# Four reorderings in a long-convolution and token-mixing kernel: weight prefetch, theta products, the pass change and the last stages

## The chip, the cores and the metric

The kernel runs on one core of one Trainium2 chip. Its time is the device time of one execution in microseconds; the median of three runs is given. The profile is one further execution recorded by the hardware profiler, whose span is a few microseconds shorter than the device time. Times inside the profile are counted from the start of that span.

Short names: PE is the matrix engine and PEld its weight loads, DVE the vector engine, ACT the scalar engine, POOL the general engine, SP the engine that here only issues transfers. A bank is one eighth of PSUM, the memory into which matmuls accumulate.

## The reference

A long convolution over the sequence (by FFT), then a token-mixing layer:

```python
# B, S, D = 8, 5696, 128
y = irfft(rfft(x, 2*S) * rfft(h, 2*S))[:, :S, :]        # convolution, per channel
theta = y @ w_theta                                     # [D, D]
zr, zi = y * cos(theta), y * sin(theta)
mix = einsum('ts,bsd->btd', w_tok_r, zr) + einsum('ts,bsd->btd', w_tok_i, zi)   # w_tok: [S, S]
u = y + mix
out = u + max(u @ w_ch, 0)                              # w_ch: [D, D]
```

Nearly all arithmetic is in the two products with the S x S weights, which are stored in float32 and read once each.

## The kernel before

**Convolution and phases.** Stages A to D are an FFT, a product and an inverse FFT in eight groups. In and after the last group, 44 *phase steps* (22 row tiles of 128, two halves of the batch) turn y into z: four transposes bring a tile of y into PSUM, DVE copies it to SBUF (`y_ap`), PE multiplies it by w_theta, ACT takes cosine and sine, DVE multiplies, and SP writes y and z to HBM. The transposes and the theta product use two halves of one PSUM tile `ps`. The first half of the batch reads its y from `ya0`. The second half reads `ya1`, whose last quarter is copied from the SBUF tile `yt` after the last inverse FFT.

```python
def stage_d(st, bp, dh):
    ...
            nc.scalar.activation(y_out, y_in, AF.Copy)
            if n0 + cn == N2:
                for e in range(2):
                    nc.sync.dma_start(yt_hbm[...], yt[64 * e:64 * e + 64]...)
...
def phase_step(ti, hh):
    ps = psum()
    tpz = ps[:, 1, :]...
    for b in range(4):
        nc.tensor.transpose(tpz[:, b, :], yT[:, b, :], ident_bf)
    y_ap = st["sby"].tile([P, 4, D], BF16, tag="y", name="y_ap")
    nc.vector.tensor_copy(y_ap, tpz)                        # DVE reads ps
    nc.sync.dma_start(y2_hbm[ti]..., y_ap...)
    phases_b(ti, y_ap, ..., theta_ps=ps[:, 0, :], tags=None)   # PE writes ps, then ACT, DVE, SP
...
load_ya1(st["yt"])          # after the last group: ya1 <- yt
...
for n, ti in enumerate(tile_order):
    phase_step(ti, 1)
    if n % 4 == 3:
        while len(bts_of[0]) < min(n // 2, NE):
            load_b(0, len(bts_of[0]), bpe)                  # operand blocks of pass 0
```

**Token mixing.** The columns of the weights are split into two passes of 2816, and 64 left over. In each pass the operand is held in SBUF as 11 blocks `b0` to `b10`, each two transfers of 512 KB; the two passes use the same SBUF space. A block holds four original parts (named by the products M2, M6, M7, M5) and three sums (M3, M4, M1). For 22 pairs of row tiles the product is made with seven matmul products in place of eight, so that the operand needs sums; two of the four parts are overwritten by sums as well. Pair 0 of each pass, the "classic" one, uses eight plain products on the original parts, and the sums are formed beside it. A last strip of 64 rows is the pair `None`. It has 88 matmuls for each pass and uses the sums in pass 0, the originals in pass 1.

```python
def sum_b(bt):
    b11, b12, b21, b22 = (bt[q] for q in (M2, M6, M7, M5))
    nc.vector.tensor_sub(bt[M3], b12, b22)
    nc.vector.tensor_sub(bt[M4], b21, b11)
    nc.vector.tensor_add(bt[M1], b11, b22)
    nc.vector.tensor_add(b12, b11, b12)      # in place
    nc.vector.tensor_add(b21, b21, b22)      # in place
...
pairs = (list(range(22)) + [None], [None] + list(range(22)))   # order in pass 0, in pass 1
```

Weights come in six buffers `wb`, each filled by four transfers that POOL issues and that turn float32 into bfloat16. A pair needs four buffers for its first 6 blocks and four for the other 5; a `None` pair needs two and two. DVE transposes them (`wt`) and forms sums of them. The work on a pair is cut into four *stretches* of 3, 3, 3 and 2 blocks.

```python
def load_w(a, row0, p, j0, nj, ng=4):
    wb = wp.tile([P, 4, CJ * 64], BF16, tag="wb")       # 6 buffers
    for i in range(4):
        nc.gpsimd.dma_start(wb[32 * i:32 * i + 32, ...], <weights, float32>)
    return wb
...
ORDER = (M3, M4, M5, M2, M1, M7, M6)                    # products of a pair, in PE's order
if tt is None:
    if first_of_pair:
        ps = [mps.tile(..., tag=f"m{q}") for q in (M3, M4)]         # banks
    ...  # 8 matmuls a block, into ps[0] and ps[1]
    if end_of_pair:
        for h in range(2):
            nc.vector.tensor_add(c[:64], c0[:64], ps[h][:64])       # frees the bank
...
if classic:
    ms = [... tag=f"m{q}" ... for q in range(4)]                    # banks m0 to m3
```

**Background and end.** While PE multiplies in pass 0, the phases of the other half of the rows run beside it. In pass 1 each finished tile gets a *u-stage*: ACT casts (`ub`), PE transposes (`utp`), ACT copies (`uts`), PE multiplies by w_ch (`v`), DVE adds (`c`), SP writes the output. `utp` and `v` share the one bank "misc". The stages still waiting at the end run after the last product:

```python
for _, first, second in spread:
    first()
    second()
```

The order of instructions on each engine is made by a scheduler from this program. It may move an instruction ahead of others on its engine where data allows it.

Of the kernel before, what the change touches and what calls it, by code (L numbers as in the profile page):

```python
# [10 lines left out]
F32 = mybir.dt.float32  # L11
# [11 lines left out]
def kernel(  # L23
# [13 lines left out]
    P = 128  # L37
# [293 lines left out]
    def stage_d(st, bp, dh):  # L331
        def chunk(n0, cn):
            if n0 == 0:
                st["yt"] = fg.tile([P, NB, N2], BF16, tag="yt", name="yt")
            g_, yt = st["g"], st["yt"]
            ps = psum()
            nq = 5 if cn == CN else cn
            for j in range(cn):
                n = n0 + j
                o = ps[:, j // nq, (j % nq) * NB:(j % nq + 1) * NB]  # L340
                for ri in range(2):
                    e_ = e_t[:K1, n, ri, :] if n < EN else e_t[:K1, N2 - n, ri, ::-1]
                    nc.tensor.matmul(o, g_[:K1, ri * N2 + n, :], e_, start=(ri == 0), stop=(ri == 1))  # L343
            y_out = yt[:, :, n0:n0 + cn].rearrange("p m (a q) -> p m a q", q=nq)
            y_in = ps[:, :cn // nq, :nq * NB].rearrange("p a (q m) -> p m a q", q=nq)
            nc.scalar.activation(y_out, y_in, AF.Copy)
            if n0 + cn == N2:
                for e in range(2):
                    nc.sync.dma_start(yt_hbm[dh * HD:(dh + 1) * HD, 2 * bp + e, :],
                                      yt[64 * e:64 * e + 64].rearrange("p m n -> p (m n)"))  # L350
        return [lambda n0=n0, cn=cn: chunk(n0, cn) for n0, cn in CHN]
# [17 lines left out]
    def phases_b(ti, y_ap, b0, nb, yT, sb, th_pool, th_tag, zi_eng, turns=None, tags=("red", "mag"), m=P,  # L369
                 theta_ps=None):  # L370
# [16 lines left out]
        else:  # L387
# [11 lines left out]
            r = theta_ps  # L399
        nc.scalar.activation(mag, r, AF.Abs)  # L400
# [70 lines left out]
    def phase_step(ti, hh):  # L471

        st = sides["phases"]
        yT = st[hh][:, :, ti * P:(ti + 1) * P]
        ps = psum()
        tpz = ps[:, 1, :].bitcast(BF16)[:, :512].rearrange("p (b t) -> p b t", b=4)
        for b in range(4):
            nc.tensor.transpose(tpz[:, b, :], yT[:, b, :], ident_bf)
        y_ap = st["sby"].tile([P, 4, D], BF16, tag="y", name="y_ap")
        nc.vector.tensor_copy(y_ap, tpz)  # L480
        nc.sync.dma_start(y2_hbm[ti].rearrange("p b d -> p (b d)")[:, 512 * hh:512 * hh + 512],
                          y_ap.rearrange("p b d -> p (b d)"))
        phases_b(ti, y_ap, 4 * hh, 4, yT, st["sb1"], None, None, nc.vector, st["turns"], theta_ps=ps[:, 0, :],
                 tags=None)
# [6 lines left out]
    for g, (bp, dh) in enumerate(groups):  # L491
# [15 lines left out]
        woven(b_, (stage_d(st, bp, dh), 0.0, 1.1 if b_ else 1.0), now)  # L507
        if g + 2 == len(groups):
            load_ya1()
    load_ya1(st["yt"])  # L510
# [24 lines left out]
    def sum_b(bt):  # L535
        b11, b12, b21, b22 = (bt[q] for q in (M2, M6, M7, M5))
        nc.vector.tensor_sub(bt[M3], b12, b22)
        nc.vector.tensor_sub(bt[M4], b21, b11)
        nc.vector.tensor_add(bt[M1], b11, b22)
        nc.vector.tensor_add(b12, b11, b12)  # L540
        nc.vector.tensor_add(b21, b21, b22)
# [15 lines left out]
    with tc.tile_pool(name="bpool", bufs=1, reuse_waits="tile") as bp, \  # L557
# [9 lines left out]
        def load_w(a, row0, p, j0, nj, ng=4):  # L567

            wb = wp.tile([P, 4, CJ * 64], BF16, tag="wb")
            for i in range(4):  # L570
                nc.gpsimd.dma_start(  # L571
                    wb[32 * i:32 * i + 32, :ng, :nj * 64],
                    bass.AP(tensor=a.tensor,
                            offset=a.offset + row0 * S + p * H + i * QR + j0 * 64,
                            ap=[[S, 32], [32 * S, ng], [1, nj * 64]]))
            return wb
# [76 lines left out]
        def u_stage(ti, h, c, m):  # L653
            st = {}

            def first():
                ub = ybp.tile([P, 4, D], BF16, tag="yb", name="ub")
                nc.scalar.activation(ub[:m].rearrange("p b d -> p (b d)"), c[:m], AF.Copy)  # L658
                utp = mps.tile([P, 4, P], BF16, tag="misc", name="utp")
                for b in range(4):  # L660
                    nc.tensor.transpose(utp[:, b, :m], ub[:m, b, :], ident_bf[:m, :m])  # L661
                st["uts"] = uts = cp.tile([P, 4, P], BF16, tag="yT", name="uts")
                nc.scalar.activation(uts[:, :, :m], utp[:, :, :m], AF.Copy)  # L663

            def second():
                v = mps.tile([P, 512], F32, tag="misc", name="v")
# [47 lines left out]
        pairs = (list(range(22)) + [None], [None] + list(range(22)))  # L714
# [8 lines left out]
        def loads(k):  # L723
# [6 lines left out]
            else:  # L730
                top, bot = tt * P, H + tt * P
                loaded[k] = [load_w(a, r, p, j0, nj) for a, r in
                             ((moe_w_tok_r, top), (moe_w_tok_i, bot),
                              (moe_w_tok_i, top), (moe_w_tok_r, bot))]

        def prepare(i, at_once=True):
# [8 lines left out]
            w11, w22, w12, w21 = loaded[k]  # L745
# [30 lines left out]
        loads(0)  # L776
        for i, (k, p, tt, j0, s0, nj) in enumerate(stretches):
            first_of_pair = j0 + s0 == 0
# [17 lines left out]
            if tt is None:  # L796


                if first_of_pair:
                    ps = [mps.tile([P, 512], F32, tag=f"m{q}", name=f"m{q}") for q in (M3, M4)]  # L800
# [4 lines left out]
                for j in range(nj):  # L805
                    jj = j0 + s0 + j
                    for r in range(2):
# [3 lines left out]
                        for h, (x0, q0, x1, q1) in enumerate(terms):  # L811
# [3 lines left out]
                                             start=False, stop=sp_)  # L815
                if end_of_pair:
# [11 lines left out]
            if first_of_pair:  # L828
                ms = [mps.tile([P, 512], F32, tag=f"m{q}", name=f"m{q}") for q in range(4 if classic else 7)]
# [20 lines left out]
            if classic:  # L850
# [10 lines left out]
                for j in range(nj):  # L861
                    sum_b(bts[j0 + s0 + j])
# [44 lines left out]
        for _, first, second in spread:  # L907
            first()
            second()
# [30 lines left out]
```

## Time and profile before

| | us |
|---|---|
| device time, median of 3 (2193.06 to 2198.13) | 2196.33 |
| span of the profile | 2192.6 |
| first matmul of pass 0 (line 856) | 555.6 |
| `None` of pass 0 begins | 1323.9 |
| first matmul of pair 0 of pass 1 (line 856) | 1383.7 |
| last vector operation begins | 2188.6 |

The engine rows of the profile give busy time, its share of the span, and the number of instructions. The window rows give, for a stretch of the span, the busy time of each engine (with the number of instructions), the granted share of PE's clock, the mean busy share of the 16 transfer engines (it can exceed 1 where packets of several queues overlap), and GB/s. In the timeline a row has start, length, engine, line, operation and tile; the brackets at its end give how long the engine had been idle before it and what ended this.

The transfer queues, from the page; the last column is the time that the packets of this queue took, as a share of 16 engines over the span:

| queue | what it carries | MB | share |
|---|---|---|---|
| q0 (issued by POOL) | weights, x | 143.00 | 48.6% |
| q1 (issued by SP) | y, z, operand blocks, results | 179.93 | 28.5% |

### The profile page before, as it was taken

The page shows a single profiled execution, that of the slowest core. Times are in us where ns is not written, and L with a number is a line of the kernel's source. Part 1 is how long each engine was busy: PE and PEld are TensorE (multiplying, and loading weights), DVE is VectorE, ACT ScalarE, POOL GpSimd, SP SyncE. Part 2 cuts the span into 40 slices and gives each one's busy share as a digit, 9 for nine tenths or more (in the row PEclk, how much of TensorE's full clock was granted, in tenths as well). Part 3 has the DMA queues.
Part 4 walks back from the last instruction along what each step waited for, and adds up shares of the span by engine and source line. Part 5 has one row for each costly group of instructions (what it writes and reads, how often), then busy time and mean ns, then how long its engine had stood idle before and what let it go on. Part 6 is the DMA issues. An engine that isn't in the chain of part 4 may idle for free.

```text
span 2192.6 us, 41307 instructions
## 1 busy us (share of the span) xinstructions
PE 2018.6 (92%) x15723; PEld 1132.8 (52%) x15723; DVE 1619.2 (74%) x2920; ACT 669.1 (31%) x984; POOL 859.3 (39%) x1568
## 2 busy tenths in 40 slices
PE   4788898756899999999999998899999999999998
PEld 3787888644344444444444443344444444444443
DVE  7766666747878888888877765677777768686866
ACT  5877777656232323323210000011111111111111
POOL 5301010020354544546466462344545353545450
PEclk8698889967999999999999999999999999999998
DMA  6356464588998989999999879677878797979793
GB/s 142 93 132 163 132 143 141 156 183 261 230 171 173 180 166 171 172 176 179 168 171 160 140 113 281 101 128 136 150 133 151 130 154 127 158 127 161 125 155 75
DMA packets 409382, 340.38 MB, mean 155 GB/s; under 512 B 83303, under 2 KB 363751, under 8 KB 408071
## 3 DMA queue, kind: packets, MB, share of 16 engines
q0 software_dynamic: 221312, 143.00, 48.6%
q1 hardware_dynamic: 183552, 179.93, 28.5%
q10 hardware_dynamic: 4320, 14.81, 1.8%
q8 instruction: 123, 2.02, 0.4%
q14 instruction: 75, 0.61, 0.1%
HBM read 381.83 MB, written 97.93 MB: 219 GB/s over the span
## 4 chain that ended last, share of the span: by engine, by line
PE 78%; DMA 7%; DVE 6%; ACT 4%; issue 2%; POOL 1%; SPq 1%; DVEq 0%; ACTq 0%; POOLq 0%
PE m L886 60%; PE m L856 4%; PE ps L320 3%; PE ps L321 3%; PE ps L190 2%; DMA hs<-hf_hbm 2%; DMA wb<-in_moe_w_tok_r_dram 2%; DVE c L893 1%; ACT xs L302 1%; PE ps L343 1%; PE ps L208 1%; DMA y_hbm<-y_ap 1%; PE utp L661 1%; PE v L668 1%; DVE u_t L304 1%
## 5 line engine op out<-in xcount | busy, mean ns | idle before, releaser
L571 POOL DMA_DIRECT2D wb<-in_moe_w_tok_i_dram x720 | 388.7, 547 | 738.7 <-DVE wt L580 660.8
L571 POOL DMA_DIRECT2D wb<-in_moe_w_tok_r_dram x720 | 387.8, 548 | 313.3 <-ACT red L401 165.3
L580 DVE STREAM_TRANSPOSE wt<-wb 128x384 f32<-128x384 f32 (+2 forms) x720 | 360.2, 523 | 125.0 <-PE m L886 67.7
L886 PE MATMUL m<-b,wt 128*128 128x512 bf16 x1848 | 426.8, 379 | 2.4 <-DVE wt L580 2.4
L886 PEld LDWEIGHTS <-wt 128*128 128x128 bf16 x1848 | 180.8, 98 | 220.8 <-DVE wt L580 3.3
L893 DVE TENSOR_TENSOR c<-c,m 128x512 f32<-128x512 f32 x420 | 270.2, 668 | 0.4 <-PE m L886 0.4
L663 ACT ACTIVATE uts<-utp 128x512 bf16<-128x512 bf16 (+1 forms) x90 | 53.3, 592 | 609.7 <-PE utp L661 609.6
L320 PE MATMUL ps<-r_u,u_t 128*128 128x128 f16 x1024 | 136.9, 231 | 16.2 <-DVE u_t L304 10.9
L321 PE MATMUL ps<-r_v,v_t 128*128 128x128 f16 x1024 | 135.6, 230 | 0.0
L658 ACT ACTIVATE ub<-c 128x512 bf16<-128x512 f32 (+1 forms) x90 | 56.3, 628 | 236.7 <-DVE c L824 151.5
L320 PEld LDWEIGHTS <-u_t 128*128 128x128 f16 x1024 | 107.8, 105 | 13.8 <-DVE u_t L304 13.8
L127 POOL DMA_DIRECT2D x<-in_x_dram x64 | 34.2, 540 | 199.2 <-PE ps L190 187.3
L321 PEld LDWEIGHTS <-v_t 128*128 128x128 f16 x1024 | 106.7, 104 | 6.7 <-issue 5.2
L302 ACT ACTIVATE xs<-ps 128x1024 f16<-128x1024 f32 x96 | 94.9, 1015 | 17.7 <-DVE v_t L304 10.3
L304 DVE TENSOR_TENSOR u_t<-xs,hs 128x1024 f16<-128x1024 f16 x96 | 68.4, 712 | 40.0 <-ACT xs L302 26.1
L190 PE MATMUL ps<-f_t,x 89*128 89x180 f16 x512 | 85.1, 312 | 8.3 <-ACT xs L302 6.2
L208 PEld LDWEIGHTS <-w_t 64*128 64x128 f16 x3240 | 64.8, 105 | 37.8 <-issue 24.7
L856 PE MATMUL m<-b,wt 128*128 128x512 bf16 x352 | 79.5, 385 | 0.7 <-ACT mag L400 0.7
L190 PEld LDWEIGHTS <-x 89*128 89x128 f16 x512 | 73.8, 237 | 10.2 <-issue 9.7
L612 ACT ACTIVATE yb<-tpz 128x512 bf16<-128x512 bf16 (+1 forms) x46 | 27.5, 597 | 153.0 <-PE tpz L610 136.1
L382 ACT ACTIVATE red<-theta_ps,magic 128x512 f32<-128x512 f32 (+1 forms) x46 | 31.6, 687 | 137.0 <-PE theta_ps L380 107.9
L304 DVE TENSOR_TENSOR v_t<-xs,hs 128x1024 f16<-128x1024 f16 x96 | 68.4, 713 | 0.0
(2712 smaller groups left out, 3791.5 us busy)
## 6 DMA issues: line engine op xcount, KB each, us to landing
wb<-in_moe_w_tok_r_dram POOLq DMA_DIRECT2D x352, 96.0 KB, 4.5
wb<-in_moe_w_tok_i_dram POOLq DMA_DIRECT2D x352, 96.0 KB, 4.8
wb<-in_moe_w_tok_r_dram POOLq DMA_DIRECT2D x352, 80.0 KB, 4.4
wb<-in_moe_w_tok_i_dram POOLq DMA_DIRECT2D x352, 80.0 KB, 3.8
hs<-hf_hbm SPq DMA_DIRECT2D x192, 128.0 KB, 3.2
cp_hbm<-c SPq DMA_DIRECT2D x88, 256.0 KB, 2.3
c<-cp_hbm SPq DMA_DIRECT2D x88, 256.0 KB, 4.5
out_dram<-c SPq DMA_DIRECT2D x88, 256.0 KB, 4.4
```

Of the source, the lines that this page charges most:

```text
L190: nc.tensor.matmul(ps[:, i // 2, (i % 2) * 2 * K1:(i % 2 + 1) * 2 * K1], lhs(q + i), f1_t[:NB], start=True, stop=True)
L208: nc.tensor.matmul(ps[:, e, j * HD:(j + 1) * HD], w_t2[rows, c0 + j, N2 * (1 - ri):N2 * (3 - ri)], a_st["a"][rows, ri * K1 + c0 + j, :], s ...
L302: nc.scalar.activation(xs[:, :, :, :ck], ps, AF.Copy)
L304: nc.vector.tensor_tensor(uv[r][:, :, :, c0:c0 + ck], xs[:, :, :, :ck], hv[:, r:r + 1, :, :ck].to_broadcast([P, 2, HD, ck]), op=mult)
L320: nc.tensor.matmul(o, u_t[:, at:at + P], r_u, start=True, stop=False)
L321: nc.tensor.matmul(o, v_t[:, at:at + P], r_v, start=False, stop=True)
L571: nc.gpsimd.dma_start(wb[32 * i:32 * i + 32, :ng, :nj * 64], bass.AP(tensor=a.tensor, offset=a.offset + row0 * S + p * H + i * QR + j0 * 6 ...
L580: nc.vector.transpose(wt.rearrange("p j t r -> p (j t r)").bitcast(F32).rearrange("p (j g t) -> p g j t", j=TJ, g=4)[:, :ng, :nj], wb[:, : ...
L658: nc.scalar.activation(ub[:m].rearrange("p b d -> p (b d)"), c[:m], AF.Copy)
L856: nc.tensor.matmul(ms[n // 2 * 2 + h], a[n][:, j, :, r], bts[jj][n % 2 * 2 + h][:, r, :], start=(n % 2 == 0 and jj == 0 and r == 0), stop= ...
L886: nc.tensor.matmul(ms[q], a[q][:, j, :, r], bts[jj][q][:, r, :], start=(jj == 0 and r == 0), stop=(jj == NJ - 1 and r == 1 and q not in left))
L893: nc.vector.tensor_tensor(c, z, ms[q], op=op)
```

## The change

It has four parts. First, the weights of the first pair are not fetched until block `b2` has landed: POOL copies two elements of it into each of these buffers before the load. Pair 0 also fetches its four weights in the order in which it uses them. Second, in a phase step the theta products come before the y copy, and `ya1` is read from `yt` before `yt` itself is written out. Third, at the pass change, `None` of pass 0 goes before pair 21, so that it no longer stands beside `None` of pass 1; the latter has banks m0 and m1 (M2, M6), pair 0 has the banks of M7, M5, M1 and M3; in pass 1 the three sums that overwrite nothing are made during `None`; and in `None` and pair 0 of pass 1 DVE keeps the order of the program. Fourth, the last four u-stages have their own banks and buffers, and all first halves come before all second halves. The aim of all four is that PE waits less between the stages.

```diff
@@ stage_d, phase_step
+                if then is not None:
+                    then(yt)                       # ya1 <- yt, ahead of yt_hbm <- yt
@@ phases_b, after the theta products
+        if copy is not None:
+            copy()
         nc.scalar.activation(mag, r, AF.Abs)
@@ phase_step
-        nc.vector.tensor_copy(y_ap, tpz)
-        nc.sync.dma_start(y2_hbm[ti]...)
+        def copy():
+            nc.vector.tensor_copy(y_ap, tpz)
+            nc.sync.dma_start(y2_hbm[ti]...)
@@ groups
-        woven(b_, (stage_d(st, bp, dh), 0.0, 1.1 if b_ else 1.0), now)
+        woven(b_, (stage_d(st, bp, dh, load_ya1 if last else None), 0.0, 1.1 if b_ else 1.0), now)
-    load_ya1(st["yt"])
@@ load_w
+            if after is not None:
+                nc.gpsimd.tensor_copy(wb[:, 0, :2], after)
@@ loads
-                             ((moe_w_tok_r, top), (moe_w_tok_i, bot),
-                              (moe_w_tok_i, top), (moe_w_tok_r, bot))]
+                after = bts_of[0][2][M2][:, 0, :2] if k == 0 else None
+                ... for n in ((0, 1, 2, 3) if tt == 0 else (0, 3, 1, 2))
@@ sums
-    def sum_b(bt):          # all five sums
+    def sums_apart(bt):     # M3, M4, M1
+    def sums_in_place(bt):  # the two in place
@@ the order of pairs
-        pairs = (list(range(22)) + [None], [None] + list(range(22)))
+        pairs = (list(range(21)) + [None, 21], [None] + list(range(22)))
@@ main loop
+            if (p, tt, j0 + s0) in ((1, None, 0), (1, 1, 0)):
+                if tt is None:
+                    ordered.enter_context(tc.manual_schedule(engines={mybir.EngineType.DVE}))
+                else:
+                    ordered.close()
-                    ps = [... for q in (M3, M4)]
+                    ps = [... for q in ((M2, M6) if p else (M3, M4))]
+                if p == 1:
+                    for j in range(nj):
+                        sums_apart(bts[j0 + s0 + j])          # in None of pass 1
-                ms = [... for q in range(4 if classic else 7)]
+                ms = [... for q in ((M7, M5, M1, M3) if classic else range(7))]
-                    sum_b(bts[j0 + s0 + j])
+                    if p == 0:
+                        sums_apart(bts[j0 + s0 + j])
+                    sums_in_place(bts[j0 + s0 + j])           # in pair 0
@@ the end
-        for _, first, second in spread:
-            first()
+        last = [(f"m{(M3, M5, M4, M2)[n % 4]}", f"m{(M5, M3, M2, M4)[n % 4]}", f"yy{n % 4}") ...]
+        for (_, first, _), tags_ in zip(spread, last):
+            first(tags_)                                     # banks of utp and v, buffer of uts
+        for _, _, second in spread:
             second()
```

## The prediction

> **What bounds the kernel now.** I read the page's engine rows first, then the chain that ended last, then windows of each stage, and last the timeline at the places where PE stood still.
>
> ```profile
> span 2192.6 us, 41307 instructions
> PE 2018.6 (92%) x15723; PEld 1132.8 (52%) x15723; DVE 1619.2 (74%) x2920; ACT 669.1 (31%) x984; POOL 859.3 (39%) x1568
> PEclk8698889967999999999999999999999999999998
> PE 78%; DMA 7%; DVE 6%; ACT 4%; issue 2%; POOL 1%; SPq 1%; DVEq 0%; ACTq 0%; POOLq 0%
> ```
>
> PE is busy for 92% and makes 78% of the chain. In the pairs, from 600 to 1320 us and from 1430 to 2170 us, PE is nearly without a gap, and no part of the change takes work from it there. So the gain must come from three seams: the phases before the first pair, the pass change, and the end. The clock row, in tenths, dips in the first quarter and nearly nowhere after.
>
> The phases, in windows (busy us with counts, then clock, share of the transfer engines, GB/s):
>
> ```profile
> 460.00:470.00 10.00, 4.20 (x46) 2.84 (x44) 5.49 (x11) 6.57 (x12) 7.44 (x14) 0.86 1.11 228
> 470.00:480.00 10.00, 2.10 (x16) 1.39 (x13) 1.88 (x3) 1.78 (x3) 3.81 (x7) 0.50 1.15 259
> 480.00:490.00 10.00, 5.18 (x28) 3.13 (x29) 1.72 (x4) 1.66 (x3) 1.63 (x3) 0.50 0.86 191
> 490.00:500.00 10.00, 8.11 (x73) 5.65 (x71) 7.44 (x15) 7.34 (x14) 0.00 (x0) 0.78 0.58 131
> 530.00:540.00 10.00, 5.07 (x47) 3.43 (x46) 8.21 (x14) 6.84 (x12) 0.00 (x0) 0.84 0.97 324
> ```
>
> From 470 to 490 us every engine rests while transfers are saturated; POOL's instructions there are the weight loads (24 of them start between 459.8 and 483.7 us). After 500 us it is transfers again: y, z and the blocks. The waits of 400 to 600 us say who stood still:
>
> ```profile
> ACT mag L400 <- PE ps L397: 57.1, 15, 15.2
> PE ps L391 <- DVE y_ap L480: 26.5, 14, 6.1
> PEld L478 <- DMA ya<-yt: 9.7, 2, 7.8
> ```
>
> The second row is the theta product that waits for the y copy, the third the second half's wait for `ya1`.
>
> The pass change:
>
> ```profile
> 1330.00:1340.00 10.00, 10.00 (x48) 5.13 (x47) 4.44 (x9) 0.00 (x0) 4.87 (x9) 1.00 1.09 368
> 1340.00:1350.00 10.00, 3.08 (x15) 1.43 (x14) 5.62 (x11) 0.00 (x0) 2.85 (x6) 0.89 1.11 341
> 1370.00:1380.00 10.00, 2.04 (x5) 0.90 (x6) 6.06 (x12) 0.00 (x0) 4.26 (x8) 0.58 0.77 161
> ...
> 1350.05 0.58 PE L812 MATMUL m<-b,wt 128*64 128x512 bf16 x1 [6.97 <-DVE c L824]
> 1373.94 1.50 DVE L580 STREAM_TRANSPOSE wt<-wb 128x384 f32<-128x384 f32 x3 [8.78 <-DMA wb<-in_moe_w_tok_r_dram]
> 1377.95 0.64 PE L814 MATMUL m<-b,wt 128*64 128x512 bf16 x1 [8.67 <-DVE wt L580]
> ```
>
> PE loses 6.97 us because `None` of pass 1 wants the banks of `None` of pass 0, whose addition (L824) stands on DVE behind sums of blocks that are still in flight. It loses 8.67 us because the transposes that it needs stand behind transposes of pair 0, whose weights had not come. At the end, DVE's rows:
>
> ```profile
> 2183.00 0.69 DVE L670 SCALAR_TENSOR_TENSOR c<-v,c 128x512 f32<-128x512 f32 x1 [2.10 <-PE v L668]
> 2185.80 0.69 DVE L670 SCALAR_TENSOR_TENSOR c<-v,c 128x512 f32<-128x512 f32 x1 [2.10 <-PE v L668]
> 2188.59 0.69 DVE L670 SCALAR_TENSOR_TENSOR c<-v,c 128x512 f32<-128x512 f32 x1 [2.10 <-PE v L668]
> ```
>
> One stage each 2.79 us: utp, uts, v and c strictly in turn through the one bank.
>
> [...] between 470 and 480 us POOL's weights and SP's writes share them at 1.15, and the y write of 481.7 us takes 6.86 us to land. So moving the weights moves their cost; it doesn't remove it. [...] after the 8.67 us gap matmuls start 0.43 us apart instead of 0.215, and the window reads 0.58.
>
> **The change part by part.**
>
> *Phases.* Rates first. Queue 0 moves 143.00 MB in 48.6% of 2192.6 us, so 7.45 us a MB; queue 1 moves 179.93 MB in 28.5%, 3.47 us a MB. The six weight buffers are 16 transfers of 96 KB and 8 of 80 KB: 2.2 MB, 16 us. A block is 1.05 MB: 3.6 us. At 460 us there remain 6 steps of the first half and 22 of the second. ACT's three functions cost 0.48 + 0.59 + 0.61 = 1.67 us a step, so 28 steps need 47 us of ACT, yet pair 0 begins at 555.6, 95 us later. With the weights out of the way and `ya1` read first, the second half should begin near 470 us and not at 489: 19 us gained. But `b2` lands some 34 us after the second half's start, so the weights fall into the stretch after 500 us, which runs at a share of 0.93. They take 16 us there, less what the present gaps (7% of 55 us) and the four loads and more that pair 0 doesn't need at once allow: 8 to 12 us given back. The order of theta and copy takes at most the 26.5 us of waits away, but most stand beside ACT or transfers; I count 2. Sum: -19 + 10 - 2 = -11, and 2 us back for pair 0's later weights, which now come while it runs. I take **-9 us**.
>
> *Pass change.* Lost now: from 1330 to 1390 us PE is idle for about 16.5 us, and some 19 matmuls at half clock cost 19 x 0.21 = 4: 20.5 us. Transfers explain when it ends: 11 blocks need 40 us, weights of `None` (0.7 MB) 5, pair 0's first four buffers 12, together 57 us from about 1326, which is 1383, where pair 0 begins. Afterwards pair 21 runs last in pass 0, and blocks 0 to 2 come free after its first stretch, so their loads begin some 26 us before pass 0 ends. Pass 0 ends at about 1343 (the same work). By then 26 us less 5 for weights have brought about six blocks. The other five (18 us) and pair 0's first weights (12 us) come during `None`'s 19.4 us and a little after. DVE has its own bound there: about 3 us of pair 21's additions, the transposes, then nine blocks of three sums at 0.61 us (16.5 us), then pair 0's first transpose: some 23 us after 1343. So pair 0 should begin between 1366 and 1372, not at 1383.7: -12 to -17, I take **-14.5**. The banks: `None` now needs M6's, the last product of pair 21, but the built order on PE puts 12 matmuls into the other bank first (2.6 us), which covers most of it.
>
> *None inside pass 0.* `None` is short (19 us) and pair 21's first four buffers (12 us) must come during it; pair 21's first product also waits for `None`'s addition. **+1 us**.
>
> *End.* The last product's addition ends at 2179.7. Then one chain remains: ub 0.6, utp 0.6, uts 0.6, v 0.6, c 0.7 = 3.1 us and some gaps, so c ends near 2183.2 and not 2189.3. Four outputs of 256 KB are then written closer together, which gives back about 1. **-5 us**.
>
> Sum: -9 - 14.5 + 1 - 5 = -27.5, so 2196.3 - 27.5 = 2169 us.
>
> **The rivals.** (1) The phases are bound by bytes, and deferring the weights gives all of the head start back. For it: the share of 0.92 over 460 to 500 and of 0.93 over 500 to 555. Against: windows at 1.11 to 1.15 show that more can be moved when several queues are full, and 480 to 500 has room. Then the phases gain 0 to 3 and the time is near 2177. (2) The fixed order on DVE becomes the bound: the sums of late blocks hold up the transposes behind them, as L824 was held up before. For it: 33 sums of 0.61 us are 20 us, as long as `None`. Against: each stretch's transposes stand one stretch ahead of the sums that could delay them. It would leave 10 us of the 20.5: near 2173. (3) Both seams overlap perfectly: pair 0 at 530 us (after 460: 28 steps with 0.39 MB of y and z each, 2.2 MB of yt and ya1, in all 13.2 MB or 46 us, then three blocks, 11, and pair 0's first weights, 12), pair 0 right after `None` at 1363, end -6. That is -25 - 20 - 6 = -51, 2145. It needs transfers without a gap. (4) A new wait in pass 0 or pair 0 that eats everything: nothing in the profile asks for it, since the added work is four POOL copies of two elements.
>
> **Range and chances.** Two of three seams would have to give almost nothing for less than -13, and both nearly all for more than -40: range 2156 to 2183. The 2% mark is 2152.4, which needs -44 of a possible 51; I give it 0.07. Slower by 2% has no mechanism: 0.01.
>
> **What would show it.** Right: pair 0 of pass 0 begins near 546; the wait of L391 for `y_ap` is gone; POOL's weight loads start near 500 us; block loads of pass 1 begin before pair 21 ends; PE's idle time from pass 0's end to pair 0 is under 9 us, with no gap that halves the clock; the last c additions stand 0.7 to 1.3 us apart. Wrong: the first matmul of pass 0 stays at 555 (rival 1), DVE waits for block transfers while PE waits for DVE (rival 2), or gaps appear inside pair 0 of pass 0 or between `None` and pair 21.

## The result and the profile after

| | before | changed |
|---|---|---|
| device time, median of 4 (us) | 2195.0 (2193.1 to 2198.1) | 2180.6 (2177.3 to 2187.7) |
| ratio, with its 95% interval | | 0.9937 (0.9908 to 0.9967) |
| span of the profile (us) | 2192.6 | 2175.5 |

The change saves 14.4 us, about half of the 27.5 us predicted. The ratio's interval lies wholly below 1, and the time lies inside the predicted range. Line numbers of the changed kernel are shifted: the classic matmuls are L878, the products L910, `None` L831 and L833, the block sums L543 to L550, the y copy L486, Abs L404.

The page of the changed kernel, its first rows, clock row and shares of the chain:

```profile
span 2175.5 us, 41105 instructions
PE 1998.2 (92%) x15545; PEld 1125.1 (52%) x15723; DVE 1619.4 (74%) x2920; ACT 670.6 (31%) x984; POOL 857.1 (39%) x1572
...
PEclk8788889987899999999999999999999999999999
...
PE 65%; DMA 5%; DVE 4%; issue 2%; ACT 2%; POOL 1%; SPq 1%; DVEq 0%; ACTq 0%; POOLq 0%
```

The work is the same: DVE's and ACT's busy times are within 2 us of before. PE's row has 178 matmuls fewer only because their records are missing from this trace (PEld still has all 15723 weight loads), and the chain through PE has holes for the same reason. So below I take PE's position from its weight loads and not from these shares. The clock row is 9 nearly everywhere after the first quarter, as before: once more the seams decide.

Windows of the phases in the changed kernel (PE, PEld, DVE, ACT, POOL busy, then clock, transfer share, GB/s):

```profile
460.00:470.00 10.00, 5.23 (x48) 3.35 (x46) 4.75 (x9) 4.05 (x8) 0.00 (x0) 0.79 0.99 254
470.00:480.00 10.00, 4.71 (x32) 3.55 (x34) 4.36 (x10) 5.14 (x9) 0.00 (x0) 0.52 0.74 190
480.00:490.00 10.00, 7.47 (x85) 5.42 (x84) 9.33 (x18) 10.00 (x19) 0.00 (x0) 1.00 0.82 186
490.00:500.00 10.00, 4.68 (x53) 3.37 (x52) 7.45 (x14) 6.23 (x12) 0.00 (x0) 1.00 0.92 269
...
510.00:520.00 10.00, 4.38 (x31) 3.61 (x33) 7.98 (x15) 5.34 (x10) 7.54 (x17) 0.51 1.12 253
520.00:530.00 10.00, 2.42 (x27) 1.62 (x24) 3.76 (x7) 1.57 (x3) 3.84 (x8) 0.84 1.14 311
530.00:540.00 10.00, 2.29 (x14) 1.57 (x14) 8.10 (x17) 6.18 (x11) 2.17 (x4) 0.50 1.11 271
540.00:550.00 10.00, 0.59 (x1) 0.36 (x3) 8.62 (x18) 2.74 (x5) 6.04 (x12) 0.50 1.12 285
```

From 460 to 500 the weights are gone: POOL is at 0.00 where it had 7.44. From 480 to 490 ACT is already busy for all of the 10 us, where it had 1.66. But from 530 on the picture of before has only moved: transfers at 1.11, PE all but idle. The rows of the waits from 400 to 600 us that answer to those of before:

```profile
ACT mag L404 <- DVE y_ap L486: 52.3, 21, 9.8
DVE b L543 <- DMA b<-z_hbm: 16.2, 9, 4.6
PE m L878 <- ACT red L405: 14.5, 1, 14.5
PEld L482 <- DMA ya<-yt: 2.1, 2, 1.7
```

The wait of the theta product for the y copy (26.5 us) is gone, and so is most of the one for `ya1` (9.7, now 2.1). ACT's Abs, which had waited 57.1 us for PE's theta product (L397), now waits almost as long, 52.3 us, for the y copy. DVE waits for blocks, and the first matmul of pair 0 waits 14.5 us until the phases' last step lets it go.

The pass change, in windows and then PE's rows where it stood still:

```profile
1340.00:1350.00 10.00, 9.76 (x45) 4.61 (x43) 7.53 (x15) 0.00 (x0) 2.69 (x5) 1.00 1.10 350
1350.00:1360.00 10.00, 7.02 (x32) 3.35 (x32) 10.00 (x20) 0.00 (x0) 2.71 (x5) 1.00 1.11 339
1360.00:1370.00 10.00, 7.38 (x24) 2.90 (x24) 7.99 (x15) 0.00 (x0) 3.23 (x6) 0.66 0.99 190
...
1350.62 0.40 PE L831 MATMUL m<-b,wt 128*64 128x512 bf16 x1 [0.52 <-DVE wt L591]
1358.89 0.38 PE L833 MATMUL m<-b,wt 128*64 128x512 bf16 x1 [2.00 <-DMA b<-z_hbm]
1363.85 0.58 PE L833 MATMUL m<-b,wt 128*64 128x512 bf16 x1 [2.01 <-DMA b<-z_hbm]
```

Two gaps of 6.97 and 8.67 us have become several of 2.0 us and less. The largest are waits for the blocks themselves, with transfers at 1.11; DVE is busy for all of 1350 to 1360. After 1363 the matmuls stand 0.43 us apart, half clock (0.55 granted from 1363.8 to 1367.4); from 1351 to 1355 they had stood 0.21 to 0.22 apart. In all PE is busy for 22.71 of the 28.5 us between the two passes, so it is idle for 5.8; before it was 24.50 of 41.0, so 16.5. The end, DVE's rows:

```profile
2166.88 1.28 DVE L917 TENSOR_TENSOR c<-c,m 128x512 f32<-128x512 f32 x2
2168.30 1.29 DVE L682 SCALAR_TENSOR_TENSOR c<-v,c 128x512 f32<-128x512 f32 x2
2170.51 1.29 DVE L682 SCALAR_TENSOR_TENSOR c<-v,c 128x512 f32<-128x512 f32 x2 [0.92 <-PE v L680]
```

The four last additions come in two couples and take 3.5 us in all, where each alone had taken 2.79.

For the comparisons I cut every trace at the same points: **A** the first Abs of the phases; **B** the first Abs of their second half; **C** the first weight load of pair 0 of pass 0; **D** of pair 2; **E** of pair 20 of pass 0; **F** of `None` of pass 1; **G** of pair 0 of pass 1; **H** of pair 2 of pass 1; **I** the last weight load of the products; **J** the end. D to E took 622.5 us in every trace of this study, and H to I 717.3 to 717.5: outside the seams nothing changes. A itself lies between 406.7 and 413.2, whatever the kernel. Lengths in us, ratios against the kernel before with their intervals:

| kernel | A–B | B–C | C–D | A–D | F–G | G–H | E–H | I–J | ratio |
|---|---|---|---|---|---|---|---|---|---|
| before | 86.0 | 59.3 | 77.2 | 222.6 | 41.0 | 76.2 | 204.6 | 15.5 | 1 |
| changed | 71.7 | 68.0 | 81.1 | 220.9 | 28.5 | 80.8 | 196.5 | 9.9 | 0.9937 (0.9908–0.9967) |
| changed, again | 72.0 | 68.7 | 79.0 | 219.8 | 27.2 | 80.8 | 195.2 | 9.9 | 0.9925 (0.9910–0.9939) |
| early steps | 71.9 | 70.2 | 79.4 | 221.5 | 28.5 | 76.2 | 191.9 | 9.9 | 0.9916 (0.9895–0.9938) |
| copy late | 67.2 | 70.5 | 78.5 | 216.2 | 27.5 | 81.1 | 195.8 | 10.1 | 0.9908 (0.9889–0.9927) |
| copy on ACT | 76.7 | 56.5 | 95.2 | 228.5 | 29.4 | 80.8 | 197.3 | 9.9 | 0.9949 (0.9928–0.9969) |
| no gate | 82.7 | 60.5 | 78.4 | 221.7 | 29.3 | 80.8 | 197.3 | 9.9 | 0.9935 (0.9914–0.9957) |
| pairs undone | 72.2 | 68.8 | 83.0 | 224.0 | 34.0 | 80.0 | 201.4 | 9.9 | 0.9955 (0.9934–0.9976) |
| early steps + copy late | 67.4 | 69.7 | 78.7 | 215.8 | 27.8 | 76.6 | 191.6 | 9.9 | 0.9877 (0.9862–0.9892) |
| ... + DVE order in phases | 67.9 | 71.1 | 93.0 | 232.1 | 26.0 | 76.2 | 189.4 | 9.9 | 0.9935 (0.9918–0.9951) |
| both, gate on `b0` | 68.1 | 71.0 | 77.6 | 216.8 | 29.9 | 76.5 | 193.6 | 9.9 | 0.9898 (0.9878–0.9918) |
| both, gate on `b4` | 67.8 | 65.8 | 87.1 | 220.7 | 27.9 | 76.6 | 191.6 | 9.9 | 0.9924 (0.9906–0.9941) |
| tail undone | 71.1 | 68.0 | 81.5 | 220.7 | 29.7 | 79.9 | 196.8 | 14.9 | 0.9951 (0.9936–0.9966) |
| free DVE order | 72.1 | 69.5 | 79.3 | 220.9 | 28.3 | 76.3 | 194.8 | 9.9 | 0.9926 (0.9903–0.9949) |

Six of these kernels run the changed phases unedited (changed, again, early steps, pairs undone, tail undone, free DVE order). Their means are A–B 71.8, B–C 68.9, C–D 80.6, A–D 221.3; B–C scatters by 2.2 us and A–D by 4.2. For the kernel before there is one trace.

### The profile page after: what moved, and what is told of

It is laid out like the page before. It is cut to its first block, busy times and chain, and to the rows that moved or that the text cites. A ratio compares the mean times of both kernels' runs of the same rounds, so it can differ in the third digit from the quotient of the medians.

```text
span 2175.5 us, 41105 instructions
## 1 busy us (share of the span) xinstructions
PE 1998.2 (92%) x15545; PEld 1125.1 (52%) x15723; DVE 1619.4 (74%) x2920; ACT 670.6 (31%) x984; POOL 857.1 (39%) x1572
## 3 DMA queue, kind: packets, MB, share of 16 engines
q1 hardware_dynamic: 183552, 179.93, 28.5%
## 4 chain that ended last, share of the span: by engine, by line
PE 65%; DMA 5%; DVE 4%; issue 2%; ACT 2%; POOL 1%; SPq 1%; DVEq 0%; ACTq 0%; POOLq 0%
PE m L910 59%; DMA b<-z_hbm 3%; PE m L878 2%; DMA z_hbm<-zz 2%; DVE c L917 1%; PE v L680 1%; PE utp L673 1%; PE m L914 1%; DVE wt L591 1%; PE m L833 1%; POOL wb L582 1%; PE m L831 1%; ACT mag L404 0%; ACT red L405 0%; PE theta_ps L382 0%
## 5 line engine op out<-in xcount | busy, mean ns | idle before, releaser
L910 PE MATMUL m<-b,wt 128*128 128x512 bf16 x1803 | 425.7, 381 | 7.1 <-DVE wt L591 2.4
L910 PEld LDWEIGHTS <-wt 128*128 128x128 bf16 x1848 | 181.3, 98 | 225.0 <-issue 5.7
L320 PE MATMUL ps<-r_u,u_t 128*128 128x128 f16 x1024 | 133.0, 228 | 14.9 <-DVE u_t L304 11.7
L320 PEld LDWEIGHTS <-u_t 128*128 128x128 f16 x1024 | 106.0, 103 | 13.6 <-DVE u_t L304 13.5
L304 DVE TENSOR_TENSOR u_t<-xs,hs 128x1024 f16<-128x1024 f16 x96 | 69.6, 725 | 41.9 <-ACT xs L302 31.5
L878 PE MATMUL m<-b,wt 128*128 128x512 bf16 x344 | 79.3, 387 | 15.3 <-ACT red L405 14.5
L190 PEld LDWEIGHTS <-x 89*128 89x128 f16 x512 | 73.8, 237 | 10.1 <-issue 9.4
```

Source lines behind the costliest of these rows:

```text
L190: nc.tensor.matmul(ps[:, i // 2, (i % 2) * 2 * K1:(i % 2 + 1) * 2 * K1], lhs(q + i), f1_t[:NB], start=True, stop=True)
L304: nc.vector.tensor_tensor(uv[r][:, :, :, c0:c0 + ck], xs[:, :, :, :ck], hv[:, r:r + 1, :, :ck].to_broadcast([P, 2, HD, ck]), op=mult)
L320: nc.tensor.matmul(o, u_t[:, at:at + P], r_u, start=True, stop=False)
L878: nc.tensor.matmul(ms[n // 2 * 2 + h], a[n][:, j, :, r], bts[jj][n % 2 * 2 + h][:, r, :], start=(n % 2 == 0 and jj == 0 and r == 0), stop= ...
L910: nc.tensor.matmul(ms[q], a[q][:, j, :, r], bts[jj][q][:, r, :], start=(jj == 0 and r == 0), stop=(jj == NJ - 1 and r == 1 and q not in left))
```

## The experiments

The theory from this profile: the phases lost their gain because ACT now waits for the y copy (the rival: bytes), and the pass change lost 4.6 us (G–H, 80.8 against 76.2) because DVE's fixed order keeps the transposes of pair 1 behind pair 0's additions.

**Early steps.** In pair 0 of pass 1, which keeps the program's order, the steps that transpose pair 1's weights move between the products.

```diff
                     aside(n == 0, n == 2)
+                    if woven and p:
+                        for n_ in {1: (0, 1), 2: (2,), 3: (3,)}.get(n, ()):
+                            step(n_)
...
-                for n_ in range(7):
+                for n_ in range(4 if p else 0, 7):
                     step(n_)
```

> One edit to the changed kernel: in pair 0 of pass 1 the first four of pair 1's transpose steps stand between the classic products in program order, and no longer behind pair 0's four c additions. Theory A (the fixed DVE order gives back 4.6 us behind pair 0 of pass 1, because pair 1's transposes wait for the c additions): the gaps of 2.49 and 1.02 us in the weight loads near 1410 us and the cold matmuls behind them go, pair 2 of pass 1 begins 3 to 4.6 us earlier against the start of pair 0, and the time falls by 3 to 4.5 us, to about 2176 to 2178. Rival B (the weights of pair 1, or the c additions themselves, hold it: the edit only moves the gap): pair 0 itself grows by 2 us or more because DVE waits inside it, and the time stays within 1 us of the changed kernel's 2180.6.

The timeline of DVE and then of PE behind pair 0 of pass 1, in the changed kernel:

```profile
1407.91 2.47 DVE L893 TENSOR_TENSOR c<-c,m 128x512 f32<-128x512 f32 x4
1410.31 1.49 DVE L591 STREAM_TRANSPOSE wt<-wb 128x384 f32<-128x384 f32 x3
...
1409.91 0.40 PE L673 MATMUL utp<-ident_bf,ub 128*128 128x128 bf16 x4 [1.91 <-ACT ub L670]
1411.06 0.23 PE L680 MATMUL v<-w_ch_sb,uts 128*128 128x128 bf16 x1 [0.75 <-ACT uts L675]
1411.34 2.29 PE L910 MATMUL m<-b,wt 128*128 128x512 bf16 x5
```

and with the early steps:

```profile
1403.73 1.49 DVE L591 STREAM_TRANSPOSE wt<-wb 128x384 f32<-128x384 f32 x3
...
1410.29 2.48 DVE L896 TENSOR_TENSOR c<-c,m 128x512 f32<-128x512 f32 x4
...
1409.36 1.03 PE L893 MATMUL m<-zl,wl 128*128 128x512 bf16 x4
1410.22 1.46 PE L913 MATMUL m<-b,wt 128*128 128x512 bf16 x6
```

In the changed kernel the transposes follow the four additions, so pair 1's first product comes at 1411.34, and its five matmuls take 2.29 us (half clock). With the edit the transposes stand 6.6 us ahead of the additions, and pair 1 follows pair 0 without a gap: six matmuls in 1.46 us. G–H is 76.2, that of before, and pair 0 has not grown. Theory A is shown: E–H is 4.6 us shorter, and G–H is 76.2 to 76.6 in all five kernels with the early steps, 79.9 to 81.1 in the seven with the fixed order and without them. The ratios against the two measurements of the changed kernel give 2.0 and 4.6 us.

**Copy late.** The y copy stands behind ACT's Abs and first Sin in program order.

```diff
-        if copy is not None:
-            copy()
         nc.scalar.activation(mag, r, AF.Abs)
         nc.scalar.activation(red, r, AF.Sin, ...)
+        if copy is not None:
+            copy()
```

> One edit to the changed kernel: the y copy on DVE stands in program order after ScalarE's Abs and first Sin, so ScalarE no longer waits for it. Theory A (the phases' gain was lost because Abs now waits for the y copy, 52.3 us of waits in all): the waits of Abs for the copy go, pair 0 of pass 0 begins 4 to 8 us earlier than 548.1, and the time falls by 3 to 7 us. Rival B (bytes set the end of the phases: a DMA share of 1.1 to 1.2 from 510 us on): pair 0 begins within 2 us of 548.1 and the time stays within 2 us of 2180.6. Rival C (the wait only changes its engine once more: the copy now waits for ScalarE, and the buffer is released later): pair 0 begins 1 to 4 us later.

The waits of Abs for the copy are gone from the list, and the time falls by 3.7 to 6.4 us (0.9908 against the two ratios of the changed kernel). But it does not come from where theory A had it: pair 0 began at 546.1, only 2.0 us earlier and not 4 to 8. A–B shrinks from 71.8 to 67.2, which is the whole gain; B–C is 70.5, not below the 68.9 of the six. In the second half ACT's waits have gone to something else, as the rows of the waits of this kernel show:

```profile
ACT mag L402 <- DVE zz L415: 33.9, 11, 9.7
PE ps L482 <- DVE y_ap L486: 27.9, 17, 10.0
DVE b L543 <- DMA b<-z_hbm: 19.8, 9, 4.6
```

So there are two answers: in the second half, where the waits had looked alarming, removing them brought nothing; in the first half the edit gained 4.6 us. How it did so there is only partly seen. Waits from 420 to 460, in the changed kernel and then with the copy late:

```profile
ACT g__8351 L325 <- PE ps L321: 9.2, 2, 8.7
...
ACT mag L404 <- DVE y_ap L486: 2.9, 4, 1.5
```

```profile
DVE y_ap L486 <- ACT red L403: 5.7, 7, 1.8
ACT g__8351 L325 <- PE ps L321: 4.0, 2, 3.9
```

Abs itself had waited only 2.9 us there. ACT's wait for a product of the transform fell from 9.2 to 4.0 (the same two numbers in the repeat of the changed kernel and in the kernel with both edits). ACT also works on the transform in this stretch, and the order in which the two kinds of work reach it has changed. No run separates the two. The new first row is the turn of the wait that rival C feared: copy and Abs read two halves of one PSUM tile, and whichever stands second in the program waited (Abs 52.3 us from 400 to 600 us in the changed kernel). Here the copy waits 5.7 us for ACT's Sin, but pair 0 did not begin later.

**Copy on ACT.** The same copy runs on ACT instead.

```diff
-            nc.vector.tensor_copy(y_ap, tpz)
+            nc.scalar.activation(y_ap, tpz, AF.Copy)
```

> One edit to the changed kernel: the y copy runs on ScalarE instead of DVE, ahead of Abs. No engine waits for another between copy and Abs then, DVE loses 44 copies of 0.42 us, and ScalarE gets 44 of about 0.45 us. Theory A (waits for DVE's copy set the pace of the second half): ScalarE's 2.1 us per step become about 2.55, the 22 steps of the second half need 56 us instead of the 85 us they take now, and pair 0 begins 5 to 12 us earlier. Rival B (bytes): within 2 us of 548.1. Rival C (ScalarE becomes the bound in the first half too, where it is busy for 19.06 of 20 us from 440 to 460): the first half ends 3 to 5 us later, and the gain shrinks to nothing or below.

A–B grows by 4.9 to 76.7, as rival C had it: with the copy on top, ACT holds up the first half (from 440 to 460 it is busy for 20.00 of 20 us). Pair 0 did begin early (543.8), but before the phases had ended, so PE alternated between them and C–D grew to 95.2. As a whole it loses: A–D 228.5.

**No gate.** The first weights wait for no block.

```diff
-                after = bts_of[0][2][M2][:, 0, :2] if k == 0 else None
+                after = None
```

> One part of the change undone: the first weight loads no longer wait for an operand block (their new order and all else stays). Prediction's reading (the gate keeps the weights' bytes out of the way of the second half's input and of the block loads): the weight loads start near 450 us instead of 511, the second half begins later by up to 10 us, pair 0 of pass 0 begins 5 to 9 us later (near 553 to 557), and the time rises by 3 to 7 us. Rival (the gate was bought back in full by its own late weights): pair 0 begins within 2 us of 548.1, and the waits of pairs 0 and 1 for weights (3.9 us given back) shrink, so that the time falls by 0 to 3 us.

POOL issues the first weights at 463.4 us and the second half begins as late as before (A–B 82.7 against 71.8 with the gate). But B–C is 60.5 against 68.9 and C–D 78.4 against 80.6, so A–D is 221.7 against 221.3, and the time is that of the changed kernel. The rival is right: the gate was bought back in full. Of its 10.9 us of head start 10.6 return, 8.4 before pair 0 and 2.2 after.

**Pairs undone** (with the changed kernel again beside it). `None` of pass 0 stands last once more.

```diff
-        pairs = (list(range(21)) + [None, 21], [None] + list(range(22)))
+        pairs = (list(range(22)) + [None], [None] + list(range(22)))
```

> The changed kernel once more, unedited, to see how far a second execution's stage times scatter and to have it beside the runs below. Expected: a ratio near 0.9937; from pair 2 of pass 0 to the last product the same length within 0.2 us; the start of pair 0 of pass 0 within 4 us of 548.1, since the runs with an identical first part have put it at 548.1 and 552.2.

> One part of the change undone: the 64-row remainder (None) of pass 0 stands last again, directly ahead of that of pass 1; own banks and the fixed DVE order stay. Prediction's reading (the earlier None lets pass 1's block loads start while pair 21 runs, and this is the main part of the pass change): the block loads start some 19 us later against the end of pass 0, pair 0 of pass 1 begins 8 to 12 us later than in the changed kernel, and the time rises by 7 to 12 us, to near the time of before. Rival (banks and DVE order bring most of it): pair 0 of pass 1 begins less than 4 us later and the time rises by under 4 us.

The repeat came out as expected (pair 0 at 551.3), except that from pair 2 to the last product it took 1.3 us less and not the same within 0.2; the 1.3 us lie in F–G. With the pairs undone F–G is 34.0 against 28.5 and 27.2, and E–H 201.4 against 196.5 and 195.2: the earlier `None` is worth 5 to 6 us. That is more than the rival allowed and less than the prediction's 8 to 12; banks, order and the split of the sums brought the other 3 of the 8 us, net of the 3.8 that the order lost behind pair 0 (G–H 80.0). The ratio agrees: 0.9955 against 0.9925, 6.6 us, of which this trace's slower pair 0 (C–D 83.0) is a part.

**Both.** Early steps and late copy together.

> The edits of the early steps and of the late y copy together. They touch different stages (pair 0 of pass 1, and the phases), so their differences from the changed kernel, 4.6 and 6.3 us by the ratios 0.9916 and 0.9908 against 0.9937, should add up: a ratio near 0.9887, 9 to 12 us below the changed kernel. If the late copy's gain was mostly scatter of the phases (its trace began pair 0 only 2.0 us earlier), the sum is 6 to 8 us.

0.9877 against 0.9925 on the same chip is 10.5 us, within the 9 to 12 expected: the two add up, A–D at 215.8 and E–H at 191.6. This version beats both kernels.

**DVE order in the phases.** On top of both, DVE keeps program order from the phases' second half to the end of pair 0 of pass 0, and the early steps hold in pass 0 too.

```diff
+    held = ExitStack()
+    held.enter_context(tc.manual_schedule(engines={mybir.EngineType.DVE}))
     for n, ti in enumerate(tile_order):
         phase_step(ti, 1)
...
+            if (p, tt, j0 + s0) == (0, 1, 0):
+                held.close()
```

> On top of the last kernel, DVE keeps program order from the second half of the phases to the end of pair 0 of pass 0, so that no block sum stands ahead of a y copy or a product of the phases; the early steps are applied at pair 0 of both passes. In the changed kernel the head start of 16 us lasts to phase step 36 of 44 (515.9 against 531.8) and is 6.8 us at step 43. Theory A (the last eight steps lose their 9 us because DVE stands in block sums that wait for block transfers, 11.3 us of such waits from 460 to 550): the last step ends 5 to 9 us earlier than in the kernel with the late copy alone (547.9), pair 0 begins by 540, and the time falls by another 2 to 6 us; pair 0 itself may grow by up to 4 us, as the sums now fall into it. Rival B (the weights' bytes slow the last steps, DMA share 1.12 to 1.18): the steps wait for their stores and buffers in place of the sums, the last step ends within 3 us of 547.9, and the time is within 2 us of the last kernel or above it.

The time rose by 12.7 us (0.9935 against 0.9877). The block sums left the phases: the first began at 553.5 us, where it had been at 496.3. Yet the phases' last steps became no faster: from the 37th Abs, step 36, to the end of the last product they took 35.3 us, against 36.3 with the sums in between. The waits of this kernel from 500 to 560 say what took their place:

```profile
DVE zz L414 <- DMA z_hbm<-zz: 28.4, 8, 9.3
...
ACT mag L402 <- DVE zz L415: 22.3, 6, 9.1
PE ps L482 <- DVE y_ap L486: 22.1, 6, 9.7
```

DVE's product waits for the z store that frees its buffer, ACT waits for DVE, and PE for both. This is rival B: the wait went on to the stores, and the engine that had been relieved gained nothing. C–D is 93.0 against 78.7, now that the sums fall into it.

**Gate on `b0` and on `b4`.** Both with early steps and late copy; only the index of the block changes.

```diff
-                after = bts_of[0][2][M2][:, 0, :2] if k == 0 else None
+                after = bts_of[0][0][M2][:, 0, :2] if k == 0 else None     # the other kernel: [4]
```

> On top of the early steps and the late copy, the first weight loads wait for the first operand block instead of the third: they start near 497 us instead of 508. Theory A (from 515 us on the phases are bound by their transfers, and the weights' bytes only cost where the DMA engines are full; from 460 to 510 their share is 0.82 to 0.88, so some 6 us of room is there): pair 0 of pass 0 begins 0 to 3 us earlier than 545.6, its own weights come earlier so that pair 2 begins 2 to 5 us earlier than 624.3, and the time falls by 1 to 4 us. Rival B (the second half's stores are what the early weights hold up, wherever they lie): steps 24 to 36 take longer than their 31.5 us, pair 2 begins within 1 us of 624.3, and the time stays within 1 us.

> On top of the early steps and the late copy, the first weight loads wait for the fifth operand block instead of the third: they start near 526 us instead of 508. Theory (the weights' bytes are what stretches the last eight steps of the phases: without them in the window the last step's product ends 26 to 27 us after step 36 begins, as before and with no gate, with them 34 to 36 us): step 36 begins near 511 as in the kernel with both edits, the last product ends 5 to 8 us earlier than 547.3, and pairs 0 and 1 wait longer for weights, so that pair 2 begins 0 to 6 us later than 624.3 and the time rises by 0 to 6 us. Rival (the stretch has another cause, such as the stores' order in the queue): the last product still ends near 547, and the time rises by 6 us or more because the weights are later and nothing is faster.

The windows of 510 to 540, first with the gate on `b2` (both edits), then on `b4`:

```profile
510.00:520.00 10.00, 6.99 (x56) 5.14 (x56) 6.65 (x13) 7.03 (x12) 7.24 (x14) 0.70 1.18 259
520.00:530.00 10.00, 1.18 (x9) 0.90 (x9) 5.84 (x10) 1.48 (x3) 3.81 (x7) 0.64 1.18 286
530.00:540.00 10.00, 1.11 (x8) 0.56 (x5) 8.68 (x19) 5.67 (x10) 1.67 (x4) 0.50 1.03 281
```

```profile
510.00:520.00 10.00, 6.87 (x55) 5.23 (x56) 8.40 (x17) 6.92 (x12) 2.04 (x7) 0.72 0.94 305
520.00:530.00 10.00, 2.00 (x14) 1.26 (x13) 7.96 (x15) 6.59 (x12) 6.44 (x13) 0.63 1.19 252
530.00:540.00 10.00, 0.00 (x0) 0.00 (x0) 6.01 (x11) 0.44 (x1) 4.04 (x8) 0.50 1.16 306
```

With `b4` POOL starts its loads at 518.5 instead of 508.0, and ACT does 6.59 us of steps from 520 to 530 where it had done 1.48. From step 36 to the last product it takes 31.8 us and not 36.3, B–C falls from 69.7 to 65.8, and then pair 0 waits for its weights: C–D is 87.1. With `b0` the weights cost their time earlier: steps 24 to 36 take 36.4 us and not 31.5, steps 36 to the end 32.7 and not 36.3. In the traces A–D grows by 1.0 and by 4.9 us; the ratios to the kernel before, 0.9898 and 0.9924 against 0.9877, say 4.6 and 10 us; for `b4` that is more than the 0 to 6 that I expected, and more than its trace shows. With `b0` theory A had expected 1 to 4 us less; its rival's sign came, the longer steps 24 to 36. The traces agree with each other: wherever the weights were put, what ran beside them took longer. The gate on `b2` was better than `b4`; against `b0` the intervals overlap (0.9862–0.9892 and 0.9878–0.9918), and 1.0 us is within the scatter of A–D.

**Tail undone** and **free DVE order.** In the first the last u-stages go one by one through "misc" again; in the second the fixed order at the pass change is dropped, and all else stays.

```diff
-        for (_, first, _), tags_ in zip(spread, last):
-            first(tags_)
-        for _, _, second in spread:
-            second()
+        for _, first, second in spread:
+            first()
+            second()
```

```diff
-            if (p, tt, j0 + s0) in ((1, None, 0), (1, 1, 0)):
+            if (p, tt, j0 + s0) in ():
```

> One part of the changed kernel undone: the last four u-stages run one after another through one bank again. Prediction's reading (the end is worth 5 us; the profile of the changed kernel puts the distance from the last product to the end of the span at 9.9 us against 15.4): the distance is near 15.4 us again and the time rises by 5 to 6 us. Rival (the fixed DVE order or the changed pair order has moved the end as well): the distance stays under 13 us.

> One part of the changed kernel undone: DVE's order at the pass change is free again; pair order, banks and the split of the block sums stay. Theory A (the fixed order wins inside the remainder, but gives 4.6 us back behind pair 0): pair 0 of pass 1 begins 3 to 8 us later after the remainder's start than its 27.2 to 28.5 us, the gap of 3.5 us behind pair 0 is gone, and the time is within 3 us of the changed kernel. Rival B (the order does nothing for the remainder, bytes do): pair 0 begins within 1.5 us of the same distance, the gap behind pair 0 is gone, and the time falls by 3 to 4.5 us, as with the early steps.

Without the tail I–J is 14.9 against 9.9, so it is worth 5.0 us; the ratios to the two measurements of the changed kernel say 3.1 and 5.7. With the free order F–G is 28.3, in the middle of what the fixed order gave in the other kernels with this order of pairs (26.0 to 29.9), and G–H is 76.3 instead of 80.8. So the fixed order did nothing for the remainder that can be seen, and gave 4.5 us away behind pair 0. E–H gains only 1.7 us, though, because pair 21 took 3.1 us longer. DVE's timeline near its end, with the free order:

```profile
1339.47 0.38 DVE L591 STREAM_TRANSPOSE wt<-wb 128x192 f32<-128x192 f32 x1
1339.78 0.65 DVE L543 TENSOR_TENSOR b<-b 128x1024 bf16<-128x1024 bf16 x1
1340.35 1.27 DVE L917 TENSOR_TENSOR c<-yy,m 128x512 f32<-128x512 bf16 x2
1341.54 0.41 DVE L600 TENSOR_TENSOR out__18262<-wt 128x512 bf16<-128x512 bf16 x1
```

The scheduler lifts block sums (L543) and transposes of pass 1 ahead of pair 21's own weight sums (L600), and PE waits for the last of these until 1342. The time did not move (0.9926). With the early steps, the fixed order is the better one: 191.9.

## Why the prediction was half right

The sum was -9 -14.5 +1 -5 = -27.5. From the table, with the mean of the six for the phases, it was -1.3 (A–D 221.3 against 222.6), -8.1 (E–H 196.5 against 204.6, with the `None` of pass 0 in it) and -5.6 (I–J): -15.0, against 14.4 measured. The errors are 7.7 us in the phases and 5.4 at the pass change.

- **Phases, -9: the term that failed.** Its first part, a head start of 19 us, was 14.2 (86.0 to 71.8), 10.9 of it by the gate. Why 4.8 us were missing no run isolates; transfers stood at 0.99 from 460 to 470 even without the weights. The 10 us given back by the deferred weights were 9.6 (59.3 to 68.9): right. The 2 us of pair 0's later weights were 3.4 (77.2 to 80.6). The 2 us for theta and copy hardly came: the kernel with no gate keeps that part and is only 0.9 us below before in A–D. ACT went on waiting, for the copy in place of the product; putting the copy behind Abs as well was what brought 4.6 us, in the first half. (The order of theta and copy was not undone alone.)

  I had counted -7 for the weights and the early `ya1` (-19 + 10 + 2); the gate, the main part of that, brought only -0.3 (-10.9 + 8.4 + 2.2). What I had written down as rival 1, that the phases are bound by bytes and gain 0 to 3 us, came near the measured size. Of the two rooms that I counted against it, 490 to 500 filled from 0.58 to 0.92, while 480 to 490 stayed (0.86, then 0.82); and from 510 to 550, where before had 0.93 to 0.97, the share rose to 1.11 to 1.14, with 253 to 311 GB/s in place of 287 to 324. (The working calls transfers saturated and every engine at rest from 470 to 490. Its own window of 480 to 490 says 0.86, with PE busy for 5.18 us.) In the kernel before, from 470 to 480 us, the packets of POOL's queue took 55.4% of the 16 engines' time and those of SP's queue 59.3%. I had written that moving the weights moves their cost, and then still let 7 us of it vanish. The runs with no gate (A–D 221.7, against 221.3 with it) and with both edits and a gate on `b0`, `b2` and `b4` (216.8, 215.8, 220.7) agree with that sentence.

  That pair 0 began at 548.1, near the 546 that I had named, is in part luck: A came 1.8 us earlier in this trace, and pairs 0 and 1 then took 3.9 us longer.
- **Pass change, -14.5: mechanism right, one step missing.** Pair 0 began at 1367.4, inside the predicted 1366 to 1372, and its 28.5 us counted from the end of pass 0 in the kernel before (1342.7) would be 1371.2, inside as well; F–G fell by 12.5 us, and PE's idle time there, 5.8 us, is under the 9 named. Whether the sums that rival 2 feared cost anything is not shown: DVE was busy without a break from 1350 to 1360, but PE's longest waits are for blocks, and the free order left F–G as it was. What no step of mine had was the far end of the fixed order: 4.6 us behind pair 0. With the early steps E–H falls by 12.7 us, near the 13.5 predicted for it and the inner `None` together. That no gap there would halve the clock was wrong: after waits of 2.00, 0.45 and 2.01 us between 1356 and 1364 it was halved (matmuls 0.43 us apart).
- **`None` inside pass 0, +1.** It cost nothing: from pair 2 of pass 0 to `None` of pass 1 it took 709.7 us instead of 709.9.
- **End, -5.** It was -5.6, and -5.0 when undone alone. The additions came in couples, 2.2 us from couple to couple.

One thing remains open. For the kernel before there is one trace, and its phases can lie as far from their mean as A–D does elsewhere (219.8 to 224.0 around 221.3). So the phases' own gain of 1.3 us is known to be small, and not better than to about 3 us either way.

## What to carry to other kernels

Where the transfer engines are near 1 or above for most of a stage (in the changed kernel 0.87 from 460 to 500 us and 1.09 from 500 to 555), a transfer moved out of the way of one wait can cost as much at the next one: of the gate's 10.9 us, 10.6 came back. Add up the bytes from the stage's start to its end before counting a head start as won. A wait of many microseconds in a list of waits is worth nothing while another one stands right behind it: removing the part of ACT's 52.3 us that lay in the second half gained nothing (B–C 70.5 against 68.9). If program order is forced on an engine, look at what the scheduler had lifted ahead at the region's far end, and put it ahead by hand; here that was worth 4.6 us.

## What the runs showed of the hardware

Between pairs 0 and 1 of pass 0 the length of a gap did not decide whether PE's clock was halved after it. The changed kernel had a gap of 2.21 us there and the kernel with both edits one of 3.04:

```profile
595.59 2.72 PE L910 MATMUL m<-b,wt 128*128 128x512 bf16 x6 [2.21 <-DVE c L893]
```

```profile
592.28 1.46 PE L913 MATMUL m<-b,wt 128*128 128x512 bf16 x6 [3.04 <-DVE c L896]
```

After the shorter one six matmuls took 2.72 us, half clock (0.51 granted from 595.5 to 599); after the longer one 1.46 us, full clock. At the same place six matmuls took 2.72 us after a gap of 3.10 (pairs undone), and 1.46 us after gaps of 2.01 (before) and 2.97 (early steps). So neither group lies above the other; what decides, no run shows. The half clock lasted for eight matmuls in the changed kernel (3.37 us in place of 1.7); with the pairs undone the first eight took 3.37 us as well, and the ninth was still slow (0.63 us long; at full clock 0.38). The difference of 3.37 and 1.7 gives an estimate: a prediction should carry some 1.7 us for a gap of 2 to 3 us as a risk.
